# Wider first products, six identity products and a new order at the start of a delta rule and mixer kernel

## The chip, the cores and the metric

The kernel runs on one core of a Trainium2 chip. Its time is the device time of one launch in microseconds (us). Work goes to five engines that run beside each other and wait for one another by semaphores: TensorE (PE, products into PSUM; its weight loads are listed apart), VectorE (DVE), ScalarE (ACT), GpSimd (POOL) and SyncE (SP, which issues DMAs). [...]

## The reference, cut to what matters

The first part is a delta rule for 4 batches and 8 heads, with 768 tokens of 48 features; the second is a mixer on the result, which has 384 features per token.

```python
k_n = k / (np.linalg.norm(k, axis=-1, keepdims=True) + 1e-06)
for t in range(S):
    y[:, :, t] = q[:, :, t] @ state                  # per batch and head
    v_old = state applied to k_n[:, :, t]
    state = state + beta * outer(k_n[:, :, t], v[:, :, t] - v_old)
x = y with the heads side by side                    # (4, 768, 384)
u = x + ((x.T @ U) @ V).T                            # over tokens, rank 32
out = u + relu(u @ w_ch1) @ w_ch2                    # 384 -> 1536 -> 384
```

All inputs and outputs are float32.

## The kernel before

**Tiling.** The tokens of a batch are cut into 12 chunks of 64. Half a batch, 6 chunks of all 8 heads, is a unit; there are 8 units, n0 to n7, and two buffers (`slots`) that they use in turn. Within a chunk the delta rule needs the inverse of a triangular 64x64 matrix built of key products. It is made of blocks of 32: each block is solved by substitution on DVE, and two blocks are joined by small products on PE. For units 0 to 2 even the 32-blocks are cut into halves of 16 for the substitution, which makes it shorter (15 steps instead of 31), and `joins` puts the halves together with two more rounds of products, called first and second here.

**A unit's stages, and their lines.** `load` (L555) brings keys, queries and values in pieces of 72 KB over the queues of SP, ScalarE and POOL. `turn` (L672) transposes key and query tiles on PE against an identity matrix, `placed` (L682 to L687) copies them out of PSUM. `products` (L700) makes the 64x64 products of keys with keys and of keys with queries, 24 at a time, on quarters of PE. Of the key products, the diagonal blocks are taken out (L710, L713), copied (L720), and for units 0 and 1 also spread into a buffer of their own (L724), which is called alone. The products of keys and queries are masked on DVE (L731), in two steps of 384 elements, one per half of the heads. `norms` (L619 to L636) takes lengths of keys from the diagonal of the transposed blocks (`gs`, L794), makes a coefficient per token (`cp`) from them and beta, copies it to the diagonal of `xt` (L627), and scales the values. `blocks` multiplies `gs` by it (L798) and runs the substitution (L803, L809), and turns the result (L816). `joins` follows on PE: first products (L860) and second products (L874), then two rounds of 32x32 products (L900 and L903, L918 and L921). `prepare` (L1023, L1034) makes what the recurrence needs, and `recur` with `outputs` (L1072, L983, L997, L1100) goes through the 12 chunks of a batch with small products that depend on each other.

**The mixer.** For each batch and each third of its tokens, `front` makes the low rank part (L1393, L1412) and transposes (L1436), `channels` multiplies by `w_ch1` (L1497) and `narrow` by `w_ch2` (L1617). The weights come by DMA and are converted by `load_weights` (L1198 on ScalarE; L1212, L1219, L1226 on DVE) before that.

**The order.** Every stage is a generator that yields what it needs and one operation at a time. Which operation comes next is not decided in the kernel: a table, `ORDER`, names the part that advances at each of 2,259 steps. It is a list written into the file. So the order on each engine is fixed by that table, the costs in `op(...)` are notes that no longer steer anything, and an engine waits wherever its next instruction isn't ready. PSUM is handed out as four pairs of banks; a stage takes one for its product and gives it back after the copy.

The first and second products of units 0 and 1 use 64x64 blocks, on two of PE's quarters, with 16 columns moving:

```python
nc.tensor.matmul(
    p_e[rows, y], of, zc[rows, e, SB:BK], start=True, stop=True
)
```

where `SB` is 16 and `BK` is 32. For unit 2 they use 32x32 blocks on four places.

## Time and profile before

| | |
|---|---|
| median of three runs | 599.55 us (595.85 to 602.98) |
| the profiled execution | 596.6 us, span 594.9 us |
| busy: PE, DVE, ACT, POOL | 559.7, 409.3, 216.8, 133.3 us |
| mean granted clock of PE | 0.943 |
| PE's first product | 9.05 us |
| unit 0: substitution begins, joins begin | 22.27, 34.19 us |
| unit 1: joins begin | 58.29 us |

The span runs from the first to the last instruction. Busy times are shares of it; matmuls are pipelined, so a busy PE isn't PE at its peak. A matmul of float32 leaves two records, a transpose one, so counts of records are twice those of products. The granted clock is the share of PE's full speed that the hardware gave it in that stretch: 1.00 or 0.50, and a value between where it changed. A row by stretches has, after its limits and length, the busy time and the number of instructions of PE, PE's weight loads, DVE, ACT and POOL, then the clock, the DMA share and GB/s. A row of waits names who waited for whom, then the us in total, how often, and the longest.

### The profile page before, as it was taken

What the parts mean: (1) busy time and instruction counts of PE and PEld (TensorE: products, weight loads), DVE (VectorE), ACT (ScalarE), POOL (GpSimd) and SP (SyncE); (2) the same over time, 40 slices, a digit from 0 to 9 for tenths busy, and PEclk for the clock granted to TensorE, in tenths of its full rate; (3) what the DMA queues carried; (4) which work ended last, traced back from release to release, by engine and by line L of the source; (5) the groups of instructions that cost most, each with busy time, mean ns of one, the idle gap of its engine ahead of it and who ended that gap; (6) DMA issues with size and microseconds to landing.
All of it is one profiled execution on the core that took longest, in us unless ns stands there. A gap on an engine that the chain in (4) does not pass through costs nothing.

```text
span 594.9 us, 23426 instructions
## 1 busy us (share of the span) xinstructions
PE 559.7 (94%) x10428; PEld 481.6 (81%) x10428; DVE 409.3 (69%) x1011; ACT 216.8 (36%) x442; POOL 133.3 (22%) x229
## 2 busy tenths in 40 slices
PE   3778978899999999999999999999999999999997
PEld 3578977678988887989889887889899868656997
DVE  3888758899999458999884279998883235313542
ACT  1846475446322542035224341252243321335000
POOL 8122036116010724141205214520310000000000
PEclk9855556999999999999999999999999999999999
DMA  9981639714030415240402144420401000000000
GB/s 140 180 176 24 214 80 197 152 56 79 3 65 12 68 31 92 46 91 13 82 2 43 18 83 90 79 56 2 95 7 43 4 2 4 16 8 1 26 28 28
DMA packets 89445, 36.23 MB, mean 61 GB/s; under 512 B 75456, under 2 KB 87104, under 8 KB 89344
## 3 DMA queue, kind: packets, MB, share of 16 engines
q1 hardware_dynamic: 80800, 24.69, 20.7%
q0 software_dynamic: 6944, 9.74, 8.3%
q8 instruction: 82, 1.34, 1.0%
q10 hardware_dynamic: 1600, 0.30, 0.3%
q14 instruction: 19, 0.16, 0.1%
HBM read 29.98 MB, written 4.72 MB: 58 GB/s over the span
## 4 chain that ended last, share of the span: by engine, by line
PE 83%; DVE 11%; issue 2%; ACT 2%; DMA 1%; SPq 0%; DVEq 0%; ACTq 0%
PE P L1617 27%; PE P L1497 22%; PE P L1296 7%; PE P L700 4%; DVE xt L809 3%; DVE prod L803 3%; PE P L1072 2%; PE P L860 2%; PE P L874 2%; PE P L1023 2%; PE P L1034 2%; PE P L983 2%; PE P L997 2%; PE P L1100 2%; PE P L1412 2%
## 5 line engine op out<-in xcount | busy, mean ns | idle before, releaser
L1497 PE MATMUL P<-ut,w_sb 128*128 128x256 f32 x648 | 150.1, 385 | 1.5 <-ACT ut L1439 0.9
L1497 PEld LDWEIGHTS P<-ut,w_sb 128*128 128x128 f32 x648 | 119.9, 190 | 18.7 <-ACT ut L1439 1.1
L1617 PE MATMUL P<-w_sb,hs 128*128 128x192 f32 x540 | 96.7, 331 | 0.1
L1617 PEld LDWEIGHTS P<-w_sb,hs 128*128 128x128 f32 x540 | 87.2, 190 | 3.7 <-issue 1.2
L809 DVE TENSOR_TENSOR xt<-xt,prod 128x112 f32<-128x112 f32 (+21 forms) x200 | 64.6, 323 | 6.9
L803 DVE TENSOR_TENSOR prod<-gs,xt 128x112 f32<-128x112 f32 (+21 forms) x200 | 63.3, 316 | 3.5
L1537 DVE TENSOR_TENSOR X<-X,P 128x192 f32<-128x192 f32 x84 | 29.1, 349 | 49.8 <-PE P L1617 49.4
L1462 ACT ACTIVATE hs<-P 128x512 f32<-128x512 f32 x54 | 32.2, 598 | 77.5 <-PE P L1497 65.6
L967 ACT COPY X<-P 64x192 f32<-64x192 f32 x96 | 30.0, 313 | 66.3 <-PE P L997 63.4
L1617 PE MATMUL P<-w_sb,S 128*128 128x192 f32 x288 | 50.7, 330 | 0.0
L1617 PEld LDWEIGHTS P<-w_sb,S 128*128 128x128 f32 x288 | 46.6, 190 | 2.8 <-issue 1.8
L555 POOL DMA_DIRECT2D slot<-in_v_dram x32 | 21.1, 664 | 92.3 <-DVE prod L803 60.3
L1085 DVE TENSOR_TENSOR z<-slot,P 128x192 f32<-128x192 f32 x44 | 15.5, 352 | 30.8 <-PE P L1072 29.7
L541 POOL DMA_DIRECT2D slot<-in_q_dram x40 | 24.6, 621 | 46.9 <-DVE slot L747 33.3
L939 ACT COPY slot<-zz 32x384 f32<-32x384 f32 x64 | 32.4, 509 | 7.0 <-DVE zz L878 3.9
L700 PE MATMUL P<-slot 48*64 48x64 f32 x1536 | 30.9, 231 | 2.1 <-issue 1.4
L1296 PE MATMUL P<-slot,w_sb 128*128 128x384 f32 x96 | 32.9, 486 | 0.0
L700 PEld LDWEIGHTS P<-slot 48*64 48x64 f32 x1536 | 27.9, 144 | 5.6 <-issue 2.7
L946 POOL MEMSET slot<- 32x384 f32 x32 | 13.3, 421 | 84.2 <-PE P L903 63.4
L1617 PE MATMUL P<-w_sb,slot 128*128 128x192 f32 x180 | 30.4, 327 | 0.9 <-DVE X L1537 0.9
L555 POOL DMA_DIRECT2D slot<-in_k_dram x44 | 29.4, 670 | 8.3 <-PE P L1100 7.6
L1617 PEld LDWEIGHTS P<-w_sb,slot 128*128 128x128 f32 x180 | 29.3, 190 | 1.7 <-DVE X L1537 1.5
(153 smaller groups left out, 901.4 us busy)
## 6 DMA issues: line engine op xcount, KB each, us to landing
out_dram<-X SPq DMA_DIRECT2D x22, 192.0 KB, 2.7
w_sb<-in_moe_w_ch_dram SPq DMA_DIRECT2D x10, 384.0 KB, 5.6
slot<-in_k_dram SPq DMA_DIRECT2D x48, 72.0 KB, 3.9
slot<-in_k_dram POOLq DMA_DIRECT2D x44, 72.0 KB, 3.8
slot<-in_v_dram SPq DMA_DIRECT2D x32, 72.0 KB, 3.7
slot<-in_v_dram POOLq DMA_DIRECT2D x32, 72.0 KB, 3.5
X<-in_moe_w_ch_dram SPq DMA_DIRECT2D x6, 384.0 KB, 6.1
wide<-in_moe_w_ch_dram SPq DMA_DIRECT2D x6, 384.0 KB, 5.0
```

Source lines behind the costliest of these rows:

```text
L541: queue.dma_start(out=blocked(n)[quarter(y % 4), j, g, :, 0:w], in_=src[b, 4 * g + 2 * j + par, hf * UC * L : (hf + 1) * UC * L, BK * low ...
L555: queue.dma_start(out=t[half(1 - g if name == "z" else g), :, to, 0:D], in_=src[b, 4 * g + s, hf * UC * L : (hf + 1) * UC * L, :].rearrang ...
L700: nc.tensor.matmul(p_g[half(g ^ (par * i)), par, c], kq[rows, c, j, 0, half(g)], kq[rows, c, j, i, half(g)], start=True, stop=True,)
L803: nc.vector.tensor_tensor(out=prod, in0=gb[:, :, j : j + 1, j + 1 :].to_broadcast([128, split, m, w]), in1=xb[:, :, 0:m, j : j + 1].to_bro ...
L809: nc.vector.tensor_tensor(out=xb[:, :, 0:m, j + 1 :], in0=xb[:, :, 0:m, j + 1 :], in1=prod, op=ALU.subtract,)
L939: nc.scalar.copy(pg[quarter(i), :, at, :, a : a + BK], cut(zc, h)[quarter(i)].rearrange("p r (c j) t -> p r c j t", j=2),)
L967: nc.scalar.copy(x[half(c % 2), c // 2, 4 * D * g : 4 * D * (g + 1)].rearrange("p (j r d) -> p r j d", r=2, d=D), states(p_y)[half(g)],)
L1296: nc.tensor.matmul(to, w, t, start=start, stop=stop, skip_group_check=True)
L1462: nc.scalar.activation(hs[:, fs[0] : fs[1] + 1 : fs[1] - fs[0]], p_f, ACTF.Relu)
L1497: nc.tensor.matmul(p_f[:, x], w(x, t), ut[:, t], start=(t == 0), stop=(t == KT - 1))
L1537: nc.vector.tensor_tensor(out=to, in0=to, in1=p, op=ALU.add)
L1617: nc.tensor.matmul(to, of[0], of[1], start=of[2], stop=of[3], skip_group_check=True)
```

## The change

The diff has five parts.

1. The first products of units 0 and 1 move all 32 columns of a block instead of the 16 that are used. The copy that follows takes the used half out of PSUM.
2. Six identity products (`filler`), 128x128 by 256 columns, are put into PE's order. Nothing reads what they write.
3. The mask of the products of keys and queries is one DVE step of 768 elements instead of two of 384.
4. The copy of the coefficients to the diagonal of `xt` moves from DVE to ScalarE as a part of its own, `spread`; the first substitution step waits for it.
5. `ORDER` is a new table of 2,257 steps.

```diff
+    FILLERS = (0, 1, 2, 3, 4, 5)
     ORDER = """
...
+    def spread(n):
+        yield op("act", 0.2)
+        nc.scalar.copy(
+            out=xt.rearrange("p s t -> p (s t)")[:, 0 : BK * BK : BK + 1], in_=cp[:, n % 2]
+        )
+        emitted(("spread", n), 0.06)
...
-        nc.vector.tensor_copy(
-            out=xt.rearrange("p s t -> p (s t)")[:, 0 : BK * BK : BK + 1], in_=cp[:, n % 2]
-        )
+        begin(spread(n), 2)
         emitted(("c", n))
...
-                for par in range(2):
-                    yield op("dve", dve(384), give=[("pair", x)] if par else ())
-                    nc.vector.tensor_tensor(
-                        out=qk[:, par, :, j],
-                        in0=p_g[:, par],
-                        in1=mask_u[:, None, :].to_broadcast([128, UC, L]),
-                        op=ALU.mult,
-                    )
+                yield op("dve", dve(768), give=[("pair", x)])
+                nc.vector.tensor_tensor(
+                    out=qk[:, :, :, j],
+                    in0=p_g,
+                    in1=mask_u[:, None, None, :].to_broadcast([128, 2, UC, L]),
+                    op=ALU.mult,
+                )
...
+        yield need(("spread", n))
         for j in range(size - 1):
...
+                at = 0 if lone else SB
...
-                        x, p_e = got, one(got)[:, 0 : 12 * SB].rearrange("p (e t) -> p e t", e=12)
+                        x, p_e = got, one(got)[:, 0 : 12 * BK].rearrange("p (e t) -> p e t", e=12)
...
                         nc.tensor.matmul(
-                            p_e[rows, y], of, zc[rows, e, SB:BK], start=True, stop=True
+                            p_e[rows, y, at:BK], of, zc[rows, e, at:BK], start=True, stop=True
                         )
...
-                nc.scalar.copy(xe, p_e)
+                nc.scalar.copy(xe, p_e[:, :, SB:BK])
...
+    def filler(k):
+        x = yield op("pe", 0.44, "F", take="pair", words=4, flow=0.427)
+        nc.tensor.matmul(
+            one(x)[:, 0:256], ident, ident[:, None, :].to_broadcast([128, 2, 128]), start=True, stop=True
+        )
+        free["pair"][x] = state["now"] + 0.06
```

In the new order of PE, the first query turn of unit 0, third before, comes after unit 0's key products. The identity products stand: one after the second turn, one after unit 0's key products, two after the first half of the betas (the third of all waits for ScalarE to free its PSUM pair), one among the recurrence of batch 0 in unit 1, and one beside the first steps of the first mixer. Unit 0's key pieces on SP's queue stand 2nd, 3rd, 6th and 7th (before 2nd, 5th, 8th and 9th), the pieces of `moe_V` 21st, 22nd, 27th and 28th (before 17th, 19th, 20th and 22nd), and the two loads of beta on POOL's queue are the 1st and 4th (before 9th and 10th). From the joins of unit 0 on, PE has the same stages in nearly the same sequence as before up to the end of batch 0's recurrence.

## The prediction

> **What bounds the kernel now.** I read the page's busy shares and slices first, then the same engines stage by stage, then the granted clock at its own steps, then TensorE's waits.

> ```profile
> span 594.9 us, 23426 instructions
> PE 559.7 (94%) x10428; PEld 481.6 (81%) x10428; DVE 409.3 (69%) x1011; ACT 216.8 (36%) x442; POOL 133.3 (22%) x229
> ...
> PEclk9855556999999999999999999999999999999999
> ```

> TensorE (PE) is busy 94% of the span, but slices 2 to 6 (30 to 105 us) run at half clock. The stages say where time can be won. In each row the first figure after the limits is the stretch, then busy time of PE, weight loads, VectorE (DVE), ScalarE, GpSimd, and the clock:

> ```profile
> 107.00:160.00 53.00, 49.90 (x1302) 41.44 (x1298) 49.50 (x108) 25.22 (x46) 14.29 (x23) 1.00 0.35 67
> 160.00:580.00 420.00, 416.92 (x6622) 353.73 (x6616) 279.34 (x703) 132.35 (x280) 80.86 (x136) 1.00 0.20 39
> ```

> From 160 us on PE idles 3 us in 420, at full clock. A new order can win almost nothing there, and loses whatever it opens. What the change can win lies before about 110 us. What is won there reaches the end, since the rest is a fixed amount of PE work; only from 107 to 160 us DVE (49.5 of 53 us) is nearly as full as PE.

> The clock changes at 24.98, 28.40, 31.81, 86.42, 93.25 and 103.49 us: the distances are 3.41, 3.41, 54.61, 6.83 and 10.24, that is 1, 1, 16, 2 and 3 times 3.413. So the clock is decided once per window of 3.413 us, by the window just ended:

> ```profile
> 18.16:21.57 3.41, 2.45 (x36) 2.05 (x36) 3.10 (x7) 2.84 (x8) 0.12 (x1) 1.00 1.10 191
> 21.57:24.98 3.41, 1.81 (x73) 1.72 (x74) 2.96 (x13) 3.41 (x7) 0.54 (x1) 1.00 1.14 176
> 28.40:31.81 3.41, 1.71 (x96) 1.44 (x92) 3.10 (x15) 0.97 (x2) 0.00 (x0) 1.00 1.22 186
> 38.64:42.05 3.41, 3.41 (x76) 3.41 (x77) 1.79 (x7) 1.43 (x4) 0.00 (x0) 0.50 0.85 154
> 52.29:55.70 3.41, 2.70 (x101) 2.52 (x99) 3.13 (x12) 1.57 (x3) 0.00 (x0) 0.50 0.20 48
> 83.01:86.42 3.41, 3.36 (x131) 3.20 (x128) 0.35 (x1) 1.79 (x5) 0.10 (x1) 0.50 0.03 5
> ```

> After 1.81 and 1.71 us of PE work the clock fell, after 2.45 it held. But 3.41 of 3.41 busy at half clock did not bring it back, and 3.36 did. The difference is how many columns move. I count records times columns times 2, a quarter of it where four 64x64 tiles work side by side (and for a lone or 32x32 product too, which is my choice). In the half-clock windows, 83.01 has 3,264 and is followed by full clock; 52.29 has 2,600 and 38.64, which holds the 16-column products, 832, and neither is. At full clock 28.40 has 2,752 and falls, one at 229.78 has 2,688 and holds. The border is near 2,700 either way, so a window at half clock must be nearly full of dense products.

> ```profile
> PE P L672 <- DMA slot<-in_k_dram: 9.4, 2, 9.1
> PE P L860 <- DVE zz L816: 2.7, 1, 2.7
> ```

> PE's two longest waits are the first key tiles and, at 34.19 us, unit 0's substitution on DVE.

> **The change, part by part.** The sum is made against the profiled execution, 596.6 us (span 594.9 and 1.7 around it). It was 2.95 us below the median of the three runs, 599.55; I take the kernel after as standing at its profiled kind of run.

> *Loads and first turns.* On SP, at some 0.65 us per issue, unit 0's key pieces stand 2nd, 3rd, 6th and 7th instead of 2nd, 5th, 8th and 9th. The first product waits for the second of them, which is issued two places (1.3 us) earlier, and its packets share full DMA engines (share 1.1 to 1.3): I take half, -0.6. A query turn (6 of the 18 products that took 4.07 us, 1.36) leaves the way of unit 0's second key half, and one identity product comes in. The nearest row for that one is the 128x256 product of L1497, 150.1 us for 324 of them, 0.46 each at full clock, to 0.93 at half: -0.4 to -0.9, I take -0.6. Betas move to the head of POOL's queue, which delays unit 1's pieces by two issues (1.3 us); PE needs these later. The pieces of moe_V go three to seven places down SP's queue, past unit 0's values; the first mixer (111 us) is the first to need them. **-1.2** (-2 to +0.5). It carries to the substitution, which starts with the last of unit 0's diagonals (18.57 us).

> *Identity products.* Four stand between 9 and 34 us, where PE is busy 17.11 of 25 us, and each adds 1,024 of my columns to a window; the three products left before the joins are the same, with one turn more. The window at 21.57 had 1,888, so one or two lift it over the border. Two are later, around the recurrence of batch 0 (the second drop, 93.25) and the first mixer. The third waits for ScalarE to free a PSUM pair, and all of PE stands behind it, but the turn that follows would need a pair too. In waits they cost nothing; if the wait that hides one is gone, 0.46. **+0.5** (0 to +2.8).

> *Joins of unit 0.* Before, they ran at half clock: 96 records of L860 in 5.30 us, 55 ns each, and L874 the same. At full clock such a product has no row. Nothing says that they gain at all (55 ns), half is the other end (28); a turn of six went from 1.45 to 0.94 and 24 dense products from about 1.67 to 0.93, ratios of 0.65 and 0.56: 0.6. The stretch from 34.19 to 46 us would shrink by 4.5. But unit 1's substitution is next on DVE, which was busy 20.5 of the 24 us from 34 to 58: no more than 3.5 can go. **-3.0** (-3.5 to 0). Here 32 columns count: 16 of them leave a window of lone products at 500 to 1,000, 32 double it, and with the dense mask and key products among them it comes near the border.

> *Joins of unit 1* (58.3 to 79.5 us). DVE makes PE wait before them; I take it that the clock is lost there, as the count of that stretch stays under the border, and they remain at half clock. Then 32 columns cost between nothing (the 64-column weight load sets the 55 ns: L860's loads are busy 10.7 of its 11.0 us) and 27 ns a record (16 more columns if the pace were columns). I take a small part: **+0.3** (0 to 2.6). If they ran at full clock, 19.47 us of PE work would be 12, but DVE is busy 17.06 of the 21.45 us: -4.

> *93.25 to 103.49.* PE busy 9.13, DVE 8.84 of 10.24 us at half clock. A full clock is worth at most DVE's idle 1.4: **-1.4** (-1.4 to 0). The window at 89.84 had 2,376; one identity product brings it to 3,400.

> *Masks and diagonals.* Two masks of 128x384 (L731, 544 ns) become one of 128x768; its row is L1417, 946: -0.14 a pair, 16 pairs, 7 of them before 160 us, where DVE is full. The diagonal copy (L627, 197 ns) leaves DVE for ScalarE, beside the scaling of L798 (590 ns in the chain) and in front of the first step, with the whole substitution behind it: hidden unless ScalarE is in an 800 ns copy, then up to 0.6 for a unit. **-0.5** (-2.6 to +1).

> *The rest of the order* has 3 us of idle to win after 160, and I put it at 0 (-1 to +2).

> The sum is -1.2 +0.5 -3.0 +0.3 -1.4 -0.5 = -5.3: **591.3 us**.

> [...]

> **The rivals.**
> - *Only the edges move.* The drop before the joins happens all the same, 1.81 and 1.71 us being far from 2.45, and the joins run at half clock as before. Start, masks, fillers and 32 columns are left: -1.2 -0.5 +0.5 +0.8 = -0.4, **596 us**. For it: 32-column lone products alone reach some 1,000 to 1,900 of the border, by how a lone product is counted, which the trace doesn't tell.
> - *The clock holds to the end.* Busy lone products count double in fact, and the joins of both units keep it: -1.2 +0.5 -3.5 -4 -1.4 -0.5, and about -2 from 79.6 to 86.4: **584.5 us**. Against it: PE must wait for unit 1's substitution.
> - *Slower: half clock with the added work paid in full.* If the drop comes before the joins, the moved columns set the pace: 192 records by 27 ns, 5.1; the six identity products stand in PE's way at 0.74 (between the two clocks' prices), 4.4; nothing is won at the start, and the window at 83.01, which passed by little, fails, so that the clock returns at 103.49: 4.60 us of PE work there become 7.7, half of it in waits, 1.5. **608 us**. It decides where the window before the joins stays below some 2 us of PE work. Against it: L860's loads fill its time.
> [...]

> **How the numbers follow.** Forecast 0.46, edges only 0.26, clock held 0.14, slower 0.14. The range leaves out the half of the held case that goes lowest and most of the slow one: 583 to 602. A measurement of this kernel tells about 1% from no change (its three runs span 595.85 to 602.98); against 599.55 that is 593.55 and 605.55. Faster by over 1%: the held case and three quarters of the forecast, 0.49. Slower by over 1%: most of the last rival, 0.13. Within: 0.38.

> **What would show it.** Clock at 1.00 when the first 64x32 product starts, and that start at 32 to 33 us; L860's answer under 45 ns a record in unit 0; unit 1's joins at 0.50; a full clock from about 85 us and no drop after; PE idle of some 3 us after 160. It is wrong if the clock at the joins is 0.50 (then 596), if the half clock lasts past 90 us, or if idle time opens behind 107 us, where DVE has no room.

## The result, and the profile after

The changed kernel takes **605.86 us** (median; 603.61 to 609.71), the kernel before beside it 598.64 us: the ratio is 1.0136 with a 95% interval of 1.0092 to 1.018. It is slower by a little over 1%. The forecast of 591.3 us is 14.6 us off, and the time lies above the range's upper end of 602. Of the 14.6 us, 7.2 are the measured loss, 5.3 the gain in the sum, and 2.0 come from the sum's starting point of 596.6 us, which lies below the median of the kernel before. The profiled execution took 603.61 us, 7.0 us more than that of before.

From the page after: the span, TensorE's line, and the granted clock by slices.

```profile
span 601.9 us, 23458 instructions
...
PE 564.6 (94%) x10440; PEld 483.7 (80%) x10440; DVE 408.9 (68%) x987; ACT 218.1 (36%) x450; POOL 133.1 (22%) x229
...
PEclk9756655999999999999999999999999999999999
```

PE is busy for 4.9 us more, and in 40 slices the clock looks much as before. The six identity products alone are 4.8 us of busy time, so PE's other work costs what it did.

The waits of PE after (who waited for whom, us in total, times, longest) tell more:

```profile
PE P L679 <- DMA slot<-in_k_dram: 6.0, 1, 6.0
PE P L707 <- ACT slot L694: 3.5, 1, 3.5
PE P L1080 <- issue: 3.3, 2, 2.6
...
PE P L679 <- issue: 1.8, 1, 1.8
PE P L868 <- DVE zz L823: 1.8, 1, 1.8
PE P L926 <- issue: 1.6, 1, 1.6
PE P L929 <- issue: 1.6, 1, 1.6
...
PE P L1005 <- issue: 1.4, 1, 1.4
...
PE P L882 <- issue: 1.0, 1, 1.0
```

Read the word "issue": PE stood still, and nothing in the profile was late. These rows add up to 11.5 us in the whole answer, against 4.7 us in the kernel before, while all other waits of PE fell from 26.6 to 21.0 us. So the accounts are: other waits -5.6, identity products +4.8, "issue" +6.8, together +6.0 of the 7.0 us. The waits that the change was to fill were filled, about one for one, and a kind of wait that the prediction had not looked at grew.

The largest of these, in the timeline of PE (start, duration, line, shape, how many, and in brackets the idle time before and its releaser):

```profile
88.06 0.86 PE L1042 MATMUL P<-slot 64*64 64x48 f32 x48
88.75 0.34 PE L1080 MATMUL P<-s,slot 48*64 48x48 f32 x9
91.67 0.36 PE L1080 MATMUL P<-s,slot 48*64 48x48 f32 x4 [2.58 <-issue]
```

A group of 16 records of L1080 stops after the ninth, stands for 2.58 us, and goes on. A product leaves two records, so the tenth belongs to a product whose first half had run: its operands were ready. What PE lacked was the tenth instruction.

### The profile page after: what moved, and what is told of

It is laid out like the page before. It is cut to its first block, busy times and chain, and to the rows that moved or that the text cites. A ratio compares the mean times of both kernels' runs of the same rounds, so it can differ in the third digit from the quotient of the medians.

```text
span 601.9 us, 23458 instructions
## 1 busy us (share of the span) xinstructions
PE 564.6 (94%) x10440; PEld 483.7 (80%) x10440; DVE 408.9 (68%) x987; ACT 218.1 (36%) x450; POOL 133.1 (22%) x229
## 4 chain that ended last, share of the span: by engine, by line
PE 84%; DVE 9%; issue 3%; DMA 1%; ACT 1%; POOL 0%; DVEq 0%; ACTq 0%; SPq 0%; POOLq 0%
PE P L1632 27%; PE P L1512 25%; PE P L1304 7%; PE P L1080 3%; PE P L707 3%; PE P L991 2%; PE P L1108 2%; PE P L1005 2%; DVE prod L810 2%; PE P L1042 2%; DVE xt L816 2%; PE P L1031 2%; PE P L882 2%; PE P L1444 1%; PE P L1420 1%
## 5 line engine op out<-in xcount | busy, mean ns | idle before, releaser
L816 DVE TENSOR_TENSOR xt<-xt,prod 128x112 f32<-128x112 f32 (+21 forms) x200 | 64.5, 323 | 6.9
L1632 PEld LDWEIGHTS P<-w_sb,S 128*128 128x128 f32 x288 | 48.5, 195 | 1.1 <-DVE X L1552 1.0
L1632 PEld LDWEIGHTS P<-w_sb,slot 128*128 128x128 f32 x180 | 29.3, 190 | 1.8 <-DVE X L1552 1.5
```

Of the source, the lines that this page charges most:

```text
L816: nc.vector.tensor_tensor(out=xb[:, :, 0:m, j + 1 :], in0=xb[:, :, 0:m, j + 1 :], in1=prod, op=ALU.subtract,)
L1632: nc.tensor.matmul(to, of[0], of[1], start=of[2], stop=of[3], skip_group_check=True)
```

## What PE waited for: lots of 256 instructions

The page lists a DMA queue for instructions, in columns of packets, MB and share of 16 engines:

```profile
q8 instruction: 82, 1.34, 1.0%
```

```
before  705  3009  4033  4289  5825  17089
after   1217  2753  3265  3521  4033  13505  18113
```

Every one of these leaves the remainder 193 when divided by 256. Over the traces of all 14 kernels of this document that holds for 113 of the 115 "issue" gaps over 0.25 us; the other two stand near 9 us, where key tiles are still arriving (here the row of L679, number 18). The gaps at the ends of lots (over 0.25 us) are 5.0 us before and 10.6 after, and this sum is used below. It goes by place, and so takes in gaps within a few records of a lot's end that the profile puts down to another engine: 0.3 us before and 0.9 after, among them the 0.6 us of L1420 at number 5055, which leaves 191. Whether these are late lots isn't shown; without them the sums are 4.7 and 9.7 us. So PE halted where a lot ended; for the largest of these gaps the times below show that the next lot had not landed yet.

From the packets of that queue, matched with the lots in order, and the records, for the lot that came late at 91.67 us:

```
lot's predecessor begins        86.52
packet of the lot sent          88.78   (2.26 later; DMA share in between 1.01)
packet landed                   90.05   (1.27)
first instruction of the lot    91.67   (1.61)
```

The next lot began 5.15 us after the one before it, whose 256 instructions were used up in 2.57 us: they were small products, and PE was at full clock from 87.57 on. Over the gaps of all runs below, this turnaround is mostly 3.1 to 3.9 us where the DMA engines are idle and 4.4 to 7.1 us where their share is over 1; the scatter is wide. Behind 230 us, where most products are the mixer's, a lot of the kernel before lasted 6.1 us (median), and of the gaps listed above one before and two after stand there. The other five of each stand at 131 us or earlier, those of before in the small products of L700, L900, L1034, L1100 and L903.

## The experiments

The ratios are to the kernel before on the same chip, whose medians were 598.8 to 599.4 us.

**1. Only the new order.** The kernel before with the table of the changed one, and none of the other four parts (steps for the parts that it lacks taken out).

```diff
-    ORDER = """  ... the order before
+    ORDER = """  ... the new order, without fillers and spread, with two steps per mask
+    FILLERS = ()
```

> The kernel after with all four edits undone: first products on 16 columns, no identity products, masks in two steps, the diagonal copied by VectorE; the new order alone is left. Supply theory (PE's instructions come in lots of 256, and the new order puts dense small products where the DMA engines are full, so that PE runs dry: 7.3 us of such gaps before 107 us in the kernel after, 3.6 before): the loss stays, 603 to 608 us, ratio 1.008 to 1.018, with 6 us or more of gaps at lot borders in all. Added work theory (the identity products, the wide products and ScalarE's copy in front of the substitution cost the time): the loss goes, 597 to 601 us, ratio 0.997 to 1.004.

Measured: 606.51 us, ratio 1.0122 (1.0087 to 1.0158). The order alone, with the lots where they end here, carries the whole loss. The gaps at the ends of lots are 9.9 us, and the one of 2.58 us stands at 89.5 us here too.

**2. Only the edits.** The order before, with 32 columns, one mask step and the diagonal on ScalarE, and no identity products.

```diff
+                yield op("dve", dve(768), give=[("pair", x)])
...
+        begin(spread(n), 2)
...
+                            p_e[rows, y, at:BK], of, zc[rows, e, at:BK], start=True, stop=True
```

> The kernel before, in its own order, with first products on 32 columns, masks in one step (at the second one's place) and the diagonal copied by ScalarE; no identity products, since the old order has no place for them. Supply theory: near the kernel before, 595 to 601 us, ratio 0.995 to 1.005, some 5 us of gaps at lot borders. Added work theory: the larger part of the loss is here, 602 to 606 us, ratio 1.006 to 1.013.

Measured: 600.9 us, ratio 1.0028 (1.0007 to 1.0049). Within 1%; the three edits, which I had put at -0.2 together, win nothing that reaches the end, and by the interval lose a little.

**3. The changed kernel with its lots moved.** 32 products of 4x4 into an unused corner of PSUM, ahead of PE's first transpose. A float32 product leaves two records and two loads here (the six identity products, L1452 after the change, are 12 of each), so PE gets 128 more instructions, and every lot ends 128 instructions earlier in the work.

```diff
+        for _ in range(32):
+            nc.tensor.matmul(P[0:4, 7, 508:512], ident[0:32, 0:4], ident[0:32, 0:4], start=True, stop=True, skip_group_check=True)
```

> The kernel after, with 32 products of 4 columns on 32 rows put ahead of PE's first transpose, where PE waits for the first keys: 128 more instructions, half a lot. No other work changes. Supply theory: gaps still stand only at lot borders, 128 instructions further back in the kernel's own stream, so at other products; the 2.6 us gap in the recurrence near 89 us and the 1.6 us gap near 447 us go or change size, and the time moves by 1.5 us or more, to 600 to 604 us if the new borders fall better, as borders taken at random would be better than the ones of the kernel after. If gaps come from waits for other engines: the same products wait, and the time stays within 1 us of the kernel after, 605 to 607 us.

Measured: 609.53 us, ratio 1.0167 (1.0142 to 1.0192). The direction was missed: I had hoped that another place would be a better one. But the gaps did move to new places (3.3 us at 68.4, 2.6 at 135.7), again at 193 of 256, and they grew to 14.5 us, with the time behind them.

**4. Identity products of 4 columns.** The same instructions in the same places, with 4 columns moving in place of 256.

```diff
-            one(x)[:, 0:256], ident, ident[:, None, :].to_broadcast([128, 2, 128]), start=True, stop=True
+            one(x)[:, 0:4], ident, ident[:, 0:4], start=True, stop=True
```

> The kernel after with its six identity products cut to 4 columns each: the instruction count, the order and the lots stay, their array work goes from 6 times 256 columns to 6 times 4. Supply theory: as the kernel after within 2 us, 604 to 608 us. If the identity products hold the clock: slower, by a half clock that comes one or two windows earlier or lasts longer, 607 to 610 us. If they cost PE time in the way of other work: faster by up to 2.8 us, 603 us.

Measured: 603.66 us, ratio 1.0069 (1.004 to 1.0098). The stretches at half clock are nearly the same ones (the joins of unit 0 begin cold, those of unit 1 warm, 64.9 us cold in all against 71.7), so the columns of the identity products did not make the clock. The time lies between the first and the third expectation: against the 1.0136 of the changed kernel it is 0.67% less, 4 us, uncertain by 3 (from the two intervals). But the kernel of experiment 1 has no identity products at all and loses 1.22%, with its lots elsewhere. So what they cost stays open.

**5 to 7. The kernel before, with its lots moved** by 64, 128 and 192 instructions. The page counts 32, 64 and 96 more products and as many loads, so the numbers of instructions in the three expectations are half of what they should say; the shifts in the names are right.

```diff
+        for _ in range(16):        # 32, 48
+            nc.tensor.matmul(P[0:4, 7, 508:512], ident[0:32, 0:4], ident[0:32, 0:4], start=True, stop=True, skip_group_check=True)
```

> The kernel before, with 16 products of 4 x 4 ahead of PE's first transpose: 32 more instructions on PE (16 weight loads, 16 products; together under 1 us, ahead of the first data), so that every border of a lot of 256 instructions falls 32 instructions earlier in the work. Theory 'supply' (PE halts where a lot ends and the next has not come): the gaps at lot borders move with the borders and their sum changes from 5.0 us; time between 597 and 606. Theory 'order' (the gaps are a matter of the work itself): gaps stay at the places of the kernel before (29.3, 74.3, 90.1, 94.8) and the time is 599.4 +- 1.

> The same with 32 products, 64 instructions earlier (with their weight loads). Supply: gaps at new places, sum other than 5.0 us, time 597 to 606; if the kernel before merely had its borders at lucky places, the mean over the three shifts is 2 us or more above 599.4; if the new order is what costs, all three stay within 2 us of 599.4.

> The same with 48 products, 96 instructions earlier. As for the two others: supply 597 to 606 with the sum of the border gaps telling the time; order: 599.4 +- 1 with gaps at the old places.

Measured: 603.73 us (1.0066, 1.0036 to 1.0097), 612.75 us (1.019, 1.0108 to 1.0272) and 605.0 us (1.008, 1.005 to 1.011). Nothing of the work changed but where its lots end, and the old order loses 4 to 14 us. The gaps stand at other products, again at 193 of 256 (the largest at 64 in L588, L1072 and L860, where they were in L700, L900 and L1100); the theory that they belong to the work falls. By time alone two gaps at 192 could pass for old ones (74.2 and 89.9 us). Some rows of the waits of PE at 128:

```profile
PE P L1034 <- issue: 3.4, 2, 1.8
...
PE P L700 <- issue: 3.1, 1, 3.1
...
PE P L983 <- issue: 2.2, 3, 1.0
```

All the gaps at the ends of lots are 15.0 us here, at other products than before. And drops of the clock come with them: this execution spends 88.7 us at half clock, with drops at 113, 137 and 158 us, each behind a window with such a gap in it; the kernel before spends 68.3. So the kernel before had its lots at a fortunate place. The added products' own work is no rival: 8, 16, 32 and 48 of them (8 is experiment 12) give 0.9943, 1.0066, 1.019 and 1.008, which doesn't go with their number. A shift by a whole lot of 256, which by this account would change nothing, wasn't run.

**8. More DMA traffic beside the work.** The kernel before with 73 more transfers of 768 packets each, between 107 and 230 us, into a tile that nothing reads.

```diff
+    sink = const.tile([128, 288], FP32, name="sink")
...
+            if 547 <= y < 910 and (y - 547) % 5 == 0:
+                z = (y - 547) // 5
+                nc.sync.dma_start(
+                    out=sink[quarter(z % 4)].rearrange("t (r d) -> t r d", r=24),
+                    in_=k[z % B, z // B % H].rearrange("(t r) d -> t r d", t=32)[:, :, 0:12],
+                )
```

> The kernel before with 73 more transfers between about 107 and 230 us, of 768 packets of 48 bytes each, into a tile that nothing reads; no instruction of PE, DVE or ACT is added. Theory 'supply under DMA load': there the lots of PE's instructions come 2.5 to 4 us after the lot before has begun, in place of about 1, and new gaps open at lot borders; +3 to +10 us. Rival 'transfers beside the work are harmless': within 1 us of 599.4.

Measured: 598.21 us, ratio 0.9982 (0.9947 to 1.0017). The row of this stretch, to be set against 0.35 for the DMA share before:

```profile
107.00:160.00 53.00, 49.79 (x1275) 42.05 (x1268) 48.77 (x111) 24.72 (x44) 14.20 (x23) 1.00 0.62 81
```

The expectation was wrong. Between 107 and 230 us the packets with instructions were sent later, by the median 1.17 us after the lot before began in place of 0.81, not 2.5 to 4. A lot lasts 5.2 us there by the median, and the gaps at the ends of lots are 4.3 us in all in this trace, 5.0 before. This much traffic beside lots of that length cost nothing that the ratio shows; the same under short lots wasn't tried.

**9 to 12. Places worked out beforehand.** From the trace of a kernel, with its gaps at lot ends taken out, I worked out what gaps there would be if the lots ended elsewhere: a turnaround of 3.15 us plus 1.3 us times the DMA share, less the time that each lot's instructions take. The two numbers are my estimate; they lie at the lower ends of the turnarounds above, 3.1 us with idle DMA engines and 4.4 with a share over 1. By this sum the changed kernel is best off 96 instructions earlier, and the kernel before better off 32 earlier than where it stands. The edit is that of 3 with 16, 24 and 48 products, and with 8 in the kernel before.

> The changed kernel with 16 products of 4 x 4 ahead of PE's first transpose (64 instructions on PE with their weight loads: a product of this type is two passes). A sum made from the changed kernel's own trace, with its border gaps taken out, each lot's borders 64 instructions earlier, and 3.15 us from the start of a lot to the first instruction of the next, plus 1.3 us times the DMA engines' busy share in the 3 us behind that start, gives 12.0 us of gaps where the unshifted kernel gets 13.8 by the same sum. Theory 'alignment' (the loss of the change is where its lots happen to end): 602 to 606. Theory 'the new order is worse at any alignment': 606 or more, as with the 128 shift before it.

> The same with 24 products, 96 instructions earlier: the best place by that sum, 8.7 us of gaps against 13.8. Alignment: 5 us less than the changed kernel, 600 to 603. The new order is worse anywhere: 605 or more.

> The same with 48 products, 192 instructions earlier: 13.5 us by the sum, so 604 to 608 by alignment; with the other theory 606 or more as well. Together with the changed kernel itself and the shifts of 64 and 128 it gives the mean of the new order over four alignments, to be set against that of the old order over the same four, 605.1 us.

> The kernel before with 8 products, 32 instructions earlier: 6.3 us by the same sum from its own trace, against 8.3 unshifted. Alignment: 596 to 599, the fastest of all; if instead the kernel before is a sharp lucky place, 601 or more as with the shifts of 64 to 192.

Measured: 602.12 us (1.0063, 1.0032 to 1.0094), **600.71 us** (1.0023, 0.9992 to 1.0055), 607.72 us (1.0124, 1.0046 to 1.0203) and **595.43 us** (0.9943, 0.9912 to 0.9975). Three times fall inside the ranges that I had made from the sum, and the last 0.6 us below its range. The gaps themselves were forecast badly. The sum had 13.8 for the changed kernel and 12.0, 8.7 and 13.5 for the three shifts, and the traces have 10.6 and 9.1, 11.0 and 17.9; it had 8.3 and 6.3 for the kernel before and its shift, and they have 5.0 and 5.3. So that the best place was picked is in part luck, and the lead of the last kernel over the kernel before isn't seen in the gaps of the two traces. Still, the theory that the new order is worse at any place falls: with 24 tiny products more, the changed kernel can't be told from the kernel before. The kernel before with 8 tiny products beats both. Its waits named "issue", all of them:

```profile
PE P L983 <- issue: 1.8, 1, 1.8
PE P L997 <- issue: 1.3, 1, 1.3
PE P L1034 <- issue: 0.6, 1, 0.6
PE P L1497 <- issue: 0.5, 1, 0.5
PE P L903 <- issue: 0.3, 1, 0.3
```

And some rows of the waits of the slowest of the four:

```profile
PE P L882 <- issue: 3.6, 2, 3.2
PE P L929 <- issue: 3.0, 2, 1.8
PE P L868 <- issue: 2.9, 2, 2.2
```

All kernels together (gaps of PE at the ends of lots, PE's time at half clock without a drop in the last microseconds, and the span, all of one execution, in us, and the ratio of many runs to the kernel before). The one execution isn't always a middle one: those of "96 earlier" and "only the edits" were the slowest of theirs, that of "more traffic" the fastest. So the gaps go with the span of their row, not with the ratio.

```
                          gaps   half clock   span    ratio
before                     5.0      68.3      594.9   1
  32 earlier               5.3      68.3      594.9   0.9943
  64 earlier              10.8      71.7      602.0   1.0066
  128 earlier             15.0      88.7      611.4   1.019
  192 earlier              8.7      78.5      602.1   1.008
  more traffic             4.3      61.4      593.6   0.9982
  only the edits           7.1      68.3      602.1   1.0028
after                     10.6      71.7      601.9   1.0136
  64 earlier               9.1      71.7      599.9   1.0063
  96 earlier              11.0      61.4      601.8   1.0023
  128 earlier             14.5      75.1      607.8   1.0167
  192 earlier             17.9      64.9      609.8   1.0124
  identity products of 4  11.0      64.9      601.9   1.0069
  only the order           9.9      71.7      604.5   1.0122
```

A straight line through the 14 spans is 589.5 us plus 1.25 times the gaps. It explains 87% of their differences, and no span is over 3.8 us off it. The 1.25 is uncertain by some 0.3, so it isn't sure that a gap costs more than its length; that one in the wrong window also costs clock is argued, from the two gaps told of below. With the time at half clock beside them in the fit, the gaps keep 1.14, so the clock alone doesn't stand in for them. Four places of the old order (0, 64, 128, 192) have a mean ratio of 1.0084, the same four of the new order 1.0123. Each mean is uncertain by some 0.0025 (from the four intervals), their difference of 0.4% by 0.35%, and four places are few: whether the new order has a cost of its own, of up to some 0.7%, stays open, and what in it, if so, wasn't tried. That the 1.0136 is for the greater part a matter of where the lots end is shown from both sides: the same order and the same work 96 instructions earlier has 1.0023, and the old order has 1.0066 to 1.019 at three other places.

## Why the prediction was wrong

**What bounds it** was read rightly as PE, with little to win behind 160 us. The sentence that a new order there "loses whatever it opens" came true, by a way that I had not priced. The rows of the same two stages after:

```profile
107.00:160.00 53.00, 50.09 (x1323) 41.15 (x1324) 48.49 (x105) 26.64 (x50) 17.27 (x29) 1.00 0.40 81
160.00:580.00 420.00, 415.08 (x6619) 351.61 (x6618) 277.89 (x686) 133.53 (x285) 84.01 (x141) 1.00 0.20 39
```

PE idles 4.9 us behind 160, where it idled 3.1. Most of the difference is one gap, again inside a group of products:

```profile
449.12 0.18 PE L926 MATMUL P<-zz 32*32 32x32 f32 x1 [1.63 <-issue]
```

**The step that failed** is "the rest of the order, 0 (-1 to +2)". The order alone, its earlier start included, costs 1.22% (0.87 to 1.58), 7 us, for the greater part through where PE's lots end: 9.9 us of gaps in its trace, 5.0 in that of the kernel before. The step asked which engine's work would come late, and it never asked whether PE's own instructions would. The view held the hint: "issue" rows with 4.7 us stood among PE's waits in the kernel before, and I passed over them. With them goes "what is won there reaches the end": what was won at the start was given back at 43, 68, 77, 82 and 92 us.

**Loads and first turns** were right in kind: the first product starts at 5.9 us in place of 9.05, and the joins of unit 0 at 32.54 in place of 34.19, 1.65 us earlier, against the 1.2 of the sum.

**Joins of unit 0**, -3.0, did not come. I had one or two identity products lift the window before them over the border. The windows of the granted clock after:

```profile
22.71:26.13 3.42, 1.51 (x49) 1.39 (x49) 3.04 (x12) 2.37 (x7) 0.00 (x0) 0.50 0.79 195
...
29.54:32.95 3.41, 1.65 (x99) 1.54 (x92) 3.38 (x8) 1.50 (x2) 0.44 (x1) 1.00 0.96 222
36.37:39.78 3.41, 3.41 (x65) 3.30 (x65) 1.41 (x5) 0.73 (x2) 0.00 (x0) 0.50 1.11 273
56.85:60.26 3.41, 3.32 (x146) 3.10 (x143) 3.31 (x6) 2.41 (x7) 0.00 (x0) 1.00 0.02 5
60.26:63.67 3.41, 2.77 (x111) 2.55 (x110) 3.38 (x10) 2.71 (x4) 0.00 (x0) 1.00 0.60 185
...
87.57:90.98 3.41, 1.51 (x101) 1.45 (x94) 2.01 (x3) 3.41 (x6) 3.21 (x6) 1.00 1.22 208
```

The grid of 3.413 us was right: after, the changes of the clock are 2, 1, 7, 2, 7, 1, 4, 101, 1 and 44 steps of 3.413 us apart. The border of 2,700 columns wasn't. In this trace windows at full clock with up to 2,544 of my columns fell and one with 2,552 held (56.85), but in the kernel before the one with 2,752 fell, as the prediction itself says, and in experiment 12 one with 3,072 (28.36). PE's busy time doesn't decide it either: 3.40 us of 3.42 fell (57.46, more traffic) and 1.79 of 3.41 held (147.69, the old order 192 earlier). What does stays open; that it is the window just ended was my inference from a few rows, and no run shows it. Besides, the work fell into other windows: PE's wait of 3.51 us for ScalarE's copy (L694) emptied one at 21 us, and in the last one before the joins (29.54) PE had 1.65 us of work, no more than the 1.71 of before. The joins ran at 0.50 from 32.95 on. This is the rival "only the edges move" for unit 0.

**Joins of unit 1** were expected at half clock and began at full: 56.85 to 63.67 is at 1.00. The answers for L868 in unit 0 and, second, in unit 1 (limits, length, busy time and records of PE and of its loads, clock):

```profile
32.50:36.30 3.80, 3.73 (x72) 3.63 (x72) 0.56 1.15 251
57.30:59.00 1.70, 1.55 (x48) 1.48 (x48) 1.00 0.00 0
```

Cold, a record with 32 columns took 52 ns, where one with 16 took 55: the wider products were free, as I took it, and the price of the rival "slower", 27 ns a record, was not paid. Warm it took 32 ns, 0.6 of the cold one, the ratio that the sum had used. But the warm stretch was short, the clock was back at full at 104.63 us in place of 103.49, to stay until 449, and nothing of it was left at the end.

**93.25 to 103.49** was to be avoided, -1.4. Half clock held from 90.98 to 104.63 instead. The last row of the windows above has what may be the reason: in it PE worked for 1.51 us, and 1.89 of the 2.58 us gap of a late lot stand in it. The next four windows were at half clock. But the kernel before lost three there, with a gap of 0.6 us at 90 us, so not all four can be put down to this gap.

**Identity products**, +0.5 (0 to +2.8): by experiment 4 about 4 us, uncertain by 3, against which experiment 1 speaks; neither the term nor its range is confirmed or refuted. **Masks and diagonals**, -0.5: with the 32 columns 1.0028 (1.0007 to 1.0049), a small loss in place of a gain.

The **rivals** asked for other clocks, and "slower" came to nearly the right time by the wrong way: its moved columns and its drop to 103.49 cost little. The 0.8 us for 32 columns in "only the edges move" had no row behind it, and by the 52 ns above they cost nothing. Neither the forecast nor a rival had an engine starved of its own instructions. All three signs of being wrong came: half clock at the joins of unit 0 (from 32.95, 0.4 us after they began), half clock past 90 us, and idle time behind 107 us. The time of 596 us that went with the first did not.

## What to carry to other kernels

Where PE's waits hold "issue" rows inside groups of products, number PE's instructions, the semaphore instructions too, and look at the remainder by the number in a packet, 256 here. It was 193 at 113 of 115 gaps here: PE waited for its own program, and shifts of 32 to 192 instructions changed where that happened. Such a kernel has to be judged at several alignments before a new order is called better or worse; here the same order spread over 2.5% (0.9943 to 1.019), more than the change. What follows from it, but wasn't tried here, is to put the ends of lots where PE works on large products or waits anyway, and to keep big loads away from stretches in which 256 instructions last less than the turnaround measured there (5.15 us at a DMA share of 1.01 for the lot at 91.67 us).

## What the runs showed of the hardware beyond that

- Between 8 and 48 products of 4x4 ahead of all work moved the kernel before between 595.4 and 612.8 us.
- Before and after, the packet of a lot was sent 0.5 us (median behind 230 us, DMA share 0.18) after the lot before it began; from 9 to 107 us, after the change, it was 1.8 us (median, share 0.62). The packet took 1.0 to 1.3 us (medians by stage), and PE's first use of a late lot came 1.2 us or more after it had landed.
- Behind a late lot of 1.63 us at 447 us, deep in the mixer, the clock was 0.50 for one window (449.38 to 452.79): the window that the gap stood in had 1.78 us of PE work. Behind one of 1.87 us at 449 us, with identity products of 4 columns, it stayed at 1.00: the window of that gap (from 446.61) had 2.30 us.
